# An attention and snake-MLP kernel: the order of the first loads and products

## The chip, the cores and the metric

The kernel runs on one core of one Trainium2 chip. The metric is device time in microseconds: the median of several runs. A core has TensorE (PE, matrix products; its weight loads are listed as PEld), VectorE (DVE), ScalarE (ACT), GpSimd (POOL) and SyncE (SP). SyncE, ScalarE and GpSimd can issue DMA transfers. In the profile, q1 is the DMA queue that SyncE fills and q0 the one that GpSimd fills.

## The reference

Linear attention over 8 batches, 8 heads, 576 positions and 64 features a head, followed by a layer of 512 to 2048 to 512 features with a "snake" activation over all 4608 positions:

```python
q_s = exp(q - max(q)) / sum(...)             # softmax over the 64 features
k_s = exp(k - max(k, axis=2)) / sum(...)     # softmax over the 576 positions
kv  = einsum('bhsd,bhse->bhde', k_s, v)      # 64 x 64 a head
x   = q_s @ kv                               # then heads side by side: 4608 x 512
h   = x @ w_in                               # 512 x 2048
g   = h + sin(alpha * h)**2 / (alpha + 1e-9)
out = g @ w_out                              # 2048 x 512, float32
```

All inputs and the output are float32.

## The kernel before

**Tiles.** The 4608 positions go in nine blocks `t` of 512 rows (`MF`); a batch is 576 rows, nine sub-blocks `j` of 64 (for the first block only the first eight sub-blocks of batch 0 are needed). q, k and v of a batch are staged with two heads' halves (`ii` = 0, 1) that can be loaded apart. `x` is kept transposed in `xT`, four chunks `c` of 128 features. `w_in` is in `win`, as four row blocks `ki` of 128 features by 2048 columns; a column block `ni` is 128 columns. It is loaded with a cast to bf16 on GpSimd's queue, in pieces `load_win(c0, c1, k0, k1)` of columns c0 to c1 and row blocks k0 to k1, each as two issues of 64 partitions (`x` = 0, 1).

**One block.** For each `ni`, `mm_h` accumulates four products (`ki` = 0 to 3) in a PSUM bank; ScalarE takes the sine of it (L260), one of three engines squares it, VectorE combines (L270), and `g` goes into 16 products per output tile (`mm_o`, L274). Products of block `t+1` run between those of block `t`.

**Order.** The schedule is manual: each engine runs its instructions in the order of the program text. Nothing reorders them, so an instruction that waits holds up everything behind it on its engine. DMAs of one queue are issued in the order of the text too, and an issue can wait for the eighth transfer before it on its queue.

**The opening** (all before 28 us), as the text orders it:

- L302: SyncE issues q half 0, k half 0, q half 1, v half 0, k half 1. `held` (L332) is a one-element copy on GpSimd that waits for a loaded piece (k half 0), so that what GpSimd issues behind it starts no earlier. Behind it come v half 1 in two pieces (sub-blocks 0 to 4 and 5 to 8), `win` in six column ranges of all four row blocks, and half of `w_out`.
- ScalarE: `exp_half` for q half 0, k half 0, q half 1 (L119), then the cast of v half 0 to `vb` (L329), the copy of the first transposed q (`qT`, L355), the exponential of k half 1, part of the cast of v half 1, an `xT` chunk (L370), the second `qT` copy (L371), and a load of the sine table.
- VectorE: `norm_q`: for each half of q the sums (L151), the reciprocals (L152) and the product (L153); then `kv_norm` (L184, L187), which writes `kbd`; the rest of the cast of v half 1; the other `xT` chunks (L369, L381).
- TensorE: `warm_up(n)` are n products whose result is not used (L343). Between them stand the transposes of normed q (L203), the K·V products `kv_mm` (L174) of each half, and the attention chunks `attn_chunk` (L231), whose output becomes `xT`. As soon as `xT` chunks 0 and 1 exist, `mm_h` runs row blocks 0 and 1 of the first two column blocks, then attention chunks 2 and 3, then row blocks 0 and 1 of column blocks 2 and 3. The row blocks 2 and 3 follow in `h_slot`, which goes through all column blocks.
- Later in block 0 SyncE loads batch 1 (`load_q1` at column blocks 6 and 13, `load_kv1` at 13, L420 and L428), and its v half 1 is cast on VectorE (L450).

Of the kernel before, what the change touches and what calls it, by code (L numbers as in the profile page):

```python
# [15 lines left out]
F32 = mybir.dt.float32  # L16
BF16 = mybir.dt.bfloat16
AX = mybir.ActivationFunctionType
ALU = mybir.AluOpType
AXL = mybir.AxisListType  # L20
# [3 lines left out]
def kernel(  # L24
# [14 lines left out]
    nc = tc.nc  # L39
    ctx.enter_context(nc.allow_non_contiguous_dma(reason="layout"))  # L40
    B, H, S, D = q.shape
# [3 lines left out]
    J = 9  # L45
# [11 lines left out]
    att1 = ctx.enter_context(tc.tile_pool(name="att1", bufs=1))  # L57
    att2 = ctx.enter_context(tc.tile_pool(name="att2", bufs=2))
    small = ctx.enter_context(tc.tile_pool(name="small", bufs=2))
# [18 lines left out]
    def src_view(t, b):  # L78
        return t[b].rearrange("(i e) (p j) d -> (e p) i (j d)", e=2, j=J)
# [5 lines left out]
    staged = {}  # L85
# [20 lines left out]
    def load_win(c0, c1, k0=0, k1=4):  # L106
        n, kk = slice(c0, c1), slice(k0, k1)
        for x in range(2):
            nc.gpsimd.dma_start(out=win[64 * x:64 * x + 64, kk, n], in_=win_v[x][:, kk, n])
# [5 lines left out]
    A = {}  # L115

    def exp_to(dst, src, iis=range(2)):
        for ii in iis:
            nc.scalar.activation(dst[:, :, ii * 128:(ii + 1) * 128].rearrange("p j (x d) -> p x j d", x=2),  # L119
                                 src[:, ii::2], AX.Exp)  # L120
# [2 lines left out]
        A["qe", b] = att2.tile([128, J, 4 * D], BF16, name="qe")  # L123
        exp_to(A["qe", b], staged["q", b])

    def exp_half(name, b, ii, j1=J):
        if ii == 0:
            A[name + "e", b] = att2.tile([128, J, 4 * D], BF16, name=name + "e")
        exp_to(A[name + "e", b][:, 0:j1], staged[name, b][:, :, 0:j1], (ii,))

    def exp_k(b):
        A["ke", b] = att2.tile([128, J, 4 * D], BF16, name="ke")
# [7 lines left out]
    def norm_q(b, engs, j1=J):  # L140

        qe = A["qe", b][:, 0:j1].rearrange("p j (ii x d) -> p ii j x d", ii=2, x=2)
        A["qn", b] = qn = att1.tile([128, 2, J, 2 * D], BF16, name="qn")
        qs = small.tile([128, J, 4], F32, name="qs")
        if len(engs) == 1:
            nc.vector.tensor_reduce(qs, A["qe", b].rearrange("p j (i d) -> p j i d", i=4), axis=AXL.X, op=ALU.add)  # L146
            nc.vector.reciprocal(qs, qs)  # L147
        for ii in range(2):
            part = qs[:, 0:j1, 2 * ii:2 * ii + 2]
            if len(engs) == 2:  # L150
                nc.vector.tensor_reduce(part, qe[:, ii], axis=AXL.X, op=ALU.add)  # L151
                nc.vector.reciprocal(part, part)  # L152
            engs[ii % len(engs)].tensor_tensor(qn[:, ii, 0:j1].rearrange("p j (x d) -> p j x d", x=2), qe[:, ii],  # L153
                                               part.unsqueeze(3).to_broadcast([128, j1, 2, D]), op=ALU.mult)
# [9 lines left out]
    def kv_mm(b, ii, pool, split=False):  # L164

        if ii == 0 or split:
            A["kvp", b] = pool.tile([128, 2, 512], F32, name="kvp", tag="a")
        kvp, ke, vt = A["kvp", b], A["ke", b], vb[b % 2]
        for j in range(J):
            for x in range(2):  # L170
                h = 2 * ii + x
                for e in range(2):
                    r = slice(64 * e, 64 * e + 64)
                    nc.tensor.matmul(kvp[64 * x:64 * x + 64, e, ii * 65:(ii + 1) * 65],  # L174
                                     ke[r, j, h * 64:(h + 1) * 64],
                                     vt[r, j, h * 65:(h + 1) * 65],
                                     start=(j == 0), stop=(j == J - 1))

    def kv_norm(b, i0=0, i1=2):

        kt, m = kbd[b % 2], i1 - i0
        kvr = small.tile([128, 2, 2], F32, name="kvr")[:, :, 0:m]
        src = A["kvp", b][:, :, i0 * 65:i1 * 65].rearrange("p e (ii c) -> p e ii c", ii=m)
        nc.vector.reciprocal(kvr, src[:, :, :, D])  # L184
        for x in range(2):
            r = slice(64 * x, 64 * x + 64)
            nc.vector.tensor_tensor(kt[r, :, i0:i1, r], src[r, :, :, 0:D],  # L187
                                    kvr[r].unsqueeze(3).to_broadcast([64, 2, m, D]), op=ALU.mult)

    def q_tile(b):  # L190
        if ("qT", b) not in A:
            A["qT", b] = att2.tile([128, 2, J, 128], BF16, name="qT")
        return A["qT", b]
# [34 lines left out]
    def attn_chunk(b, c, j0, j1, xp):  # L228

        ii, e = divmod(c, 2)  # L230
        nc.tensor.matmul(xp, kbd[b % 2][:, e, ii], A["qT", b][:, ii, j0:j1, e * 64:(e + 1) * 64],  # L231
                         start=True, stop=True)
# [7 lines left out]
    def bank(kind):  # L240

        if kind == "k":
            return ps_k.tile([128, 2, MF], F32, name="kvp", tag="a")[:, 0]
        pool = {"a": lambda: ps_h[0], "b": lambda: ps_h[1], "l": lambda: ps_l, "o": lambda: ps_o}[kind]()
        return pool.tile([128, MF], F32, name={"l": "lp", "o": "op"}.get(kind, "hp"), tag=kind)

    def mm_h(t, ni, k0=0, k1=4):

        if ni == 0 and k0 == 0:
            G[t] = gpool.tile([128, nN, MF], BF16, name="g")  # L250
        hp = HP[t, ni] if k0 else bank(BANKS.get(t, 4 * "aabb")[ni])
        HP[t, ni] = hp
        for ki in range(k0, k1):
            nc.tensor.matmul(hp, win[:, ki, ni * 128:(ni + 1) * 128],  # L254
                             xT[:, ki, t * MF % NX:t * MF % NX + MF], start=(ki == 0), stop=(ki == 3))
        return hp
# [36 lines left out]
    ACT_CP, DVE_CP, GP_CP = nc.scalar.copy, nc.vector.tensor_copy, nc.gpsimd.tensor_copy  # L293
    V, GP = nc.vector, nc.gpsimd
# [3 lines left out]
    def load0(eng, n, t, ii, j0=0, j1=J):  # L298
        eng.dma_start(out=staged[n, 0][:, ii::2, j0:j1].rearrange("p i j d -> p i (j d)"),  # L299
                      in_=src_view(t, 0)[:, ii::2, j0 * D:j1 * D])  # L300

    for n, t, ii in (("q", q, 0), ("k", k, 0), ("q", q, 1), ("v", v, 0), ("k", k, 1)):  # L302
        load0(nc.sync, n, t, ii, 0, 8 if n == "q" else J)
    nc.scalar.dma_start(out=alpha_rows, in_=moe_alpha.rearrange("(no ni) -> no ni", ni=128))
    make_identity(nc, ident)
# [23 lines left out]
        eng(vv[:, 2 * ii:2 * ii + 2, j0:j1, 0:D], staged["v", 0][:, ii::2, j0:j1])  # L329

    held = singles.tile([128, 1], F32, name="held")
    GP_CP(held, staged["k", 0][:, 0, 0, 0:1])  # L332
    load0(GP, "v", v, 1, 0, 5)
    load0(GP, "v", v, 1, 5, 9)
    for c0, c1 in ((0, 256), (256, 512), (512, 768), (768, 1024), (1024, 1536), (1536, 2048)):
        load_win(c0, c1)
    for c in range(2):
        load_wout(4 * c, 4 * c + 4)
# [1 line left out]
    def warm_up(n):  # L340

        for _ in range(n):
            nc.tensor.matmul(warm, identb, A["qe", 0][:, 0:4, 0:128], start=True, stop=True)  # L343

    exp_half("q", 0, 0, 8)
    exp_half("k", 0, 0)
    exp_half("q", 0, 1, 8)
    warm_up(7)  # L350
    norm_q(0, [V, V], 8)
    q_tile(0)
    q_transpose_ii(0, 0, 0, 8, tp0)
    cast_v0(0, 0, 9, ACT_CP)
# [1 line left out]
    exp_half("k", 0, 1)  # L356
    warm_up(2)
    kv_mm(0, 0, ps_k, split=True)
    warm_up(3)
    kv_norm(0, 0, 1)  # L360
    tp1 = ps_l.tile([128, 8, 128], BF16, name="tp", tag="l")
    q_transpose_ii(0, 1, 0, 8, tp1)
# [12 lines left out]
    for ki in range(2):  # L375
        for ni in range(2):
            mm_h(0, ni, ki, ki + 1)
    for c in range(2, 4):
        xp = bank("l")
        attn_chunk(0, c, 0, 8, xp)  # L380
        DVE_CP(xT[:, c, 0:MF], xp)  # L381
    for ki in range(2):
        for ni in range(2, 4):
            mm_h(0, ni, ki, ki + 1)

    def h_slot(t, ni, sq, lag):
        hp = mm_h(t, ni, 2 if ni < (4, 1, 0)[min(t, 2)] else 0)
# [161 lines left out]
    c0 = J * 2 * P  # L549
# [30 lines left out]
    for t in range(3, nT):  # L580
        b = t + 1 if t + 1 < B else None
# [60 lines left out]
```

## Time and profile before

| what | value |
|---|---|
| median of 3 runs | 284.21 us (284.12 to 284.5) |
| the profiled execution's own time | 283.31 us |
| its span, first to last instruction | 281.5 us |
| TensorE busy | 270.0 us, 96% |
| ScalarE busy | 225.3 us, 80% |
| VectorE busy | 188.8 us, 67% |
| GpSimd busy | 83.5 us, 30% |
| granted TensorE clock, mean | 1.000 |
| read from and written to HBM | 36.71 and 9.44 MB |

The span is what the profile shows, and 1.8 us of the profiled execution's time lie around it. Shares of busy time are means over stages; the rows of a stage say what that stage waits for. A row of the timeline is start, length, engine, line, operation, tiles written and read, form and count; a bracket at its end gives the idle time ahead of it and what ended that.

### The profile page before, as it was taken

The page shows a single profiled execution, that of the slowest core. Times are in us where ns is not written, and L with a number is a line of the kernel's source. Part 1 is how long each engine was busy: PE and PEld are TensorE (multiplying, and loading weights), DVE is VectorE, ACT ScalarE, POOL GpSimd, SP SyncE. Part 2 cuts the span into 40 slices and gives each one's busy share as a digit, 9 for nine tenths or more (in the row PEclk, how much of TensorE's full clock was granted, in tenths as well). Part 3 has the DMA queues.
Part 4 walks back from the last instruction along what each step waited for, and adds up shares of the span by engine and source line. Part 5 has one row for each costly group of instructions (what it writes and reads, how often), then busy time and mean ns, then how long its engine had stood idle before and what let it go on. Part 6 is the DMA issues. An engine that isn't in the chain of part 4 may idle for free.

```text
span 281.5 us, 4812 instructions
## 1 busy us (share of the span) xinstructions
PE 270.0 (96%) x1828; PEld 128.3 (46%) x1857; DVE 188.8 (67%) x286; ACT 225.3 (80%) x320; POOL 83.5 (30%) x80
## 2 busy tenths in 40 slices
PE   2999999999999999999999999999999999999994
PEld 1444444444444444444444444444444444444443
DVE  4968678899877768766875678577765555555412
ACT  4989477999489999899989998999877777777400
POOL 2989411877666450115003501250000000000000
PEclk9999999999999999999999999999999999999999
DMA  7999989898599039712991199109011111112143
GB/s 265 299 199 232 299 282 334 329 307 302 118 235 386 8 82 330 292 37 49 269 380 43 29 296 376 28 10 161 11 29 37 37 40 37 37 37 45 42 103 75
DMA packets 39127, 45.80 MB, mean 163 GB/s; under 512 B 17072, under 2 KB 22464, under 8 KB 39104
## 3 DMA queue, kind: packets, MB, share of 16 engines
q1 hardware_dynamic: 33360, 40.57, 47.2%
q0 software_dynamic: 5552, 4.79, 10.2%
q8 instruction: 14, 0.23, 0.3%
q10 hardware_dynamic: 192, 0.14, 0.2%
q14 instruction: 9, 0.07, 0.1%
HBM read 36.71 MB, written 9.44 MB: 164 GB/s over the span
## 4 chain that ended last, share of the span: by engine, by line
PE 85%; DMA 7%; POOL 2%; DVE 2%; issue 1%; ACT 1%; SPq 1%; ACTq 0%
PE op L274 38%; PE hp L254 37%; DMA st_v<-in_v_dram 4%; PE xp L223 2%; DMA win<-in_moe_w_in_dram 2%; DMA st_k<-in_k_dram 2%; PE kvp L174 2%; PE lp L254 2%; POOL s L264 1%; PE op L612 1%; PE op L254 1%; ACT s L260 1%; PE kvp L254 1%; POOL st_v L299 1%; DVE g L270 1%
## 5 line engine op out<-in xcount | busy, mean ns | idle before, releaser
L270 DVE SCALAR_TENSOR_TENSOR g<-s,inva_sb,hp 128x512 bf16<-128x512 f32 x128 | 94.1, 745 | 58.1 <-ACT s L262 52.6
L254 PE MATMUL hp<-xT,win 128*128 128x512 bf16 x507 | 127.7, 379 | 0.7 <-DMA win<-in_moe_w_in_dram 0.5
L274 PE MATMUL op<-wout,g 128*128 128x512 bf16 x477 | 121.6, 379 | 1.4 <-issue 0.6
L260 ACT ACTIVATE s<-hp,alpha_sb 128x512 f32<-128x512 f32 x128 | 86.2, 682 | 23.1 <-PE hp L254 22.3
L254 PEld LDWEIGHTS <-win 128*128 128x128 bf16 x576 | 56.0, 98 | 67.7 <-issue 1.3
L274 PEld LDWEIGHTS <-g 128*128 128x128 bf16 x560 | 54.0, 98 | 61.0 <-DVE g L270 0.3
L262 ACT ACTIVATE s<-s 128x512 f32<-128x512 f32 x112 | 70.5, 630 | 3.5
L264 POOL TENSOR_TENSOR s<-s 128x512 f32<-128x512 f32 x29 | 30.4, 1063 | 20.1 <-ACT s L260 20.0
L153 POOL TENSOR_TENSOR qn<-qe,qs 128x1152 bf16<-128x1152 bf16 (+1 forms) x12 | 25.1, 2110 | 33.6 <-DVE qs L147 22.3
L286 DVE COPY o<-op 128x512 f32<-128x512 f32 (+2 forms) x33 | 22.1, 669 | 9.9 <-PE op L274 5.5
L138 POOL CAST vb<-st_v 128x1152 bf16<-128x1152 f32 x12 | 14.4, 1233 | 46.0 <-DMA st_v<-in_v_dram 32.0
L119 ACT ACTIVATE qe<-st_q 128x1152 bf16<-128x1152 f32 (+1 forms) x16 | 17.5, 1130 | 5.8 <-DMA st_q<-in_q_dram 5.6
L119 ACT ACTIVATE ke<-st_k 128x1152 bf16<-128x1152 f32 x16 | 17.9, 1151 | 1.3 <-DMA st_k<-in_k_dram 1.3
L146 DVE TENSOR_REDUCE qs<-qe 128x36 f32<-128x2304 bf16 x5 | 12.8, 2553 | 7.9 <-ACT qe L119 7.9
L226 DVE CAST xT<-xp 128x512 bf16<-128x512 f32 (+1 forms) x18 | 13.5, 751 | 0.0
L151 DVE TENSOR_REDUCE qs<-qe 128x16 f32<-128x1024 bf16 (+1 forms) x6 | 7.5, 1252 | 4.9 <-ACT qe L119 4.9
L119 ACT ACT_TABLE_LOAD x7 | 9.0, 1283 | 1.3 <-PEq L626 1.2
L274 PE MATMUL lp<-wout,g 128*128 128x512 bf16 x31 | 8.8, 379 | 0.2 <-issue 0.2
L274 PE MATMUL hp<-wout,g 128*128 128x512 bf16 x30 | 8.6, 380 | 0.1
L223 PE MATMUL xp<-qT,kbd 128*128 128x256 bf16 (+1 forms) x40 | 8.2, 286 | 0.0
L187 DVE TENSOR_TENSOR kbd<-kvp,kvr 64x256 bf16<-64x256 f32 (+1 forms) x20 | 7.4, 369 | 0.5
L174 PEld LDWEIGHTS <-ke 64*64 64x64 bf16 x576 | 5.7, 106 | 4.2 <-ACT vb L329 1.1
(83 smaller groups left out, 135.3 us busy)
## 6 DMA issues: line engine op xcount, KB each, us to landing
out_dram<-o SPq DMA_DIRECT2D x70, 128.0 KB, 2.4
st_q<-in_q_dram SPq DMA_DIRECT2D x6, 1152.0 KB, 6.6
st_k<-in_k_dram SPq DMA_DIRECT2D x6, 1152.0 KB, 8.7
st_v<-in_v_dram SPq DMA_DIRECT2D x6, 1152.0 KB, 11.5
st_k<-in_k_dram SPq DMA_DIRECT2D x4, 576.0 KB, 7.1
st_q<-in_q_dram SPq DMA_DIRECT2D x4, 512.0 KB, 5.7
st_v<-in_v_dram SPq DMA_DIRECT2D x3, 576.0 KB, 7.9
wout<-in_moe_w_out_dram POOLq DMA_DIRECT2D x3, 512.0 KB, 10.3
```

Of the source, the lines that this page charges most:

```text
L119: nc.scalar.activation(dst[:, :, ii * 128:(ii + 1) * 128].rearrange("p j (x d) -> p x j d", x=2), src[:, ii::2], AX.Exp)
L138: engs[ii](vv[:, 2 * ii:2 * ii + 2, :, 0:D], staged["v", b][:, ii::2])
L153: engs[ii % len(engs)].tensor_tensor(qn[:, ii, 0:j1].rearrange("p j (x d) -> p j x d", x=2), qe[:, ii], part.unsqueeze(3).to_broadcast([12 ...
L223: nc.tensor.matmul(xp[:, e, 0:n], kt[:, e, ii], qT[:, ii, j0:j1, e * 64:(e + 1) * 64], start=True, stop=True)
L226: eng(xT[:, 2 * ii:2 * ii + 2, c0:c0 + n], xp[:, :, 0:n])
L254: nc.tensor.matmul(hp, win[:, ki, ni * 128:(ni + 1) * 128], xT[:, ki, t * MF % NX:t * MF % NX + MF], start=(ki == 0), stop=(ki == 3))
L260: nc.scalar.activation(s, hp, AX.Sin, scale=alpha_sb[:, ni:ni + 1])
L262: nc.scalar.activation(s, s, AX.Square)
L264: nc.gpsimd.tensor_tensor(s, s, s, op=ALU.mult)
L270: nc.vector.scalar_tensor_tensor(G[t][:, ni], in0=s, scalar=inva_sb[:, ni:ni + 1], in1=hp, op0=ALU.mult, op1=ALU.add)
L274: nc.tensor.matmul(acc, G[t][:, ni, j * 128:(j + 1) * 128], wout[:, ni, :], start=(ni == 0), stop=(ni == nN - 1))
L286: eng(o[:, cols], acc)
```

## The change

Four edits in the opening.

- v half 1 of batch 0 becomes the sixth load on SyncE's queue, as one transfer, and leaves GpSimd's. GpSimd's gate waits for q half 1 rather than k half 0.
- The first 512 columns of `win` are loaded by half of the row blocks: row blocks 0 and 1 of columns 0 to 255, the same of columns 256 to 511, then row blocks 2 and 3 of columns 0 to 511. The other columns stay as they are.
- The exponentials of each q half of batch 0 are taken in two parts of four sub-blocks, and the sums (new `norm_q0`) in the same parts; reciprocal and product stay one instruction a half.
- On TensorE the second group of warm-up products behind the first K·V products is one instead of three, and row block 0 of column blocks 2 and 3 stands ahead of attention chunks 2 and 3.

```diff
-    def exp_half(name, b, ii, j1=J):
-        if ii == 0:
+    def exp_half(name, b, ii, j1=J, j0=0):
+        if (name + "e", b) not in A:
             A[name + "e", b] = att2.tile([128, J, 4 * D], BF16, name=name + "e")
-        exp_to(A[name + "e", b][:, 0:j1], staged[name, b][:, :, 0:j1], (ii,))
+        exp_to(A[name + "e", b][:, j0:j1], staged[name, b][:, :, j0:j1], (ii,))
...
-    for n, t, ii in (("q", q, 0), ("k", k, 0), ("q", q, 1), ("v", v, 0), ("k", k, 1)):
+    for n, t, ii in (("q", q, 0), ("k", k, 0), ("q", q, 1), ("v", v, 0), ("k", k, 1), ("v", v, 1)):
         load0(nc.sync, n, t, ii, 0, 8 if n == "q" else J)
...
-    GP_CP(held, staged["k", 0][:, 0, 0, 0:1])
-    load0(GP, "v", v, 1, 0, 5)
-    load0(GP, "v", v, 1, 5, 9)
-    for c0, c1 in ((0, 256), (256, 512), (512, 768), (768, 1024), (1024, 1536), (1536, 2048)):
+    GP_CP(held, staged["q", 0][:, 1, 0, 0:1])
+    for c0, c1, k0 in ((0, 256, 0), (256, 512, 0), (0, 512, 2)):
+        load_win(c0, c1, k0, k0 + 2)
+    for c0, c1 in ((512, 768), (768, 1024), (1024, 1536), (1536, 2048)):
         load_win(c0, c1)
...
-    exp_half("q", 0, 0, 8)
+    qe0 = A["qe", 0] = att2.tile([128, J, 4 * D], BF16, name="qe")
+    qn0 = A["qn", 0] = att1.tile([128, 2, J, 2 * D], BF16, name="qn")
+    qs0 = small.tile([128, J, 4], F32, name="qs")
+
+    def norm_q0(ii):
+        part = qs0[:, 0:8, 2 * ii:2 * ii + 2]
+        src = qe0[:, 0:8, ii * 128:(ii + 1) * 128].rearrange("p j (x d) -> p j x d", x=2)
+        for j0 in (0, 4):
+            nc.vector.tensor_reduce(part[:, j0:j0 + 4], src[:, j0:j0 + 4], axis=AXL.X, op=ALU.add)
+        nc.vector.reciprocal(part, part)
+        nc.vector.tensor_tensor(qn0[:, ii, 0:8].rearrange("p j (x d) -> p j x d", x=2), src,
+                                part.unsqueeze(3).to_broadcast([128, 8, 2, D]), op=ALU.mult)
+
+    for j0 in (0, 4):
+        exp_half("q", 0, 0, j0 + 4, j0)
     exp_half("k", 0, 0)
-    exp_half("q", 0, 1, 8)
+    for j0 in (0, 4):
+        exp_half("q", 0, 1, j0 + 4, j0)
     warm_up(7)
-    norm_q(0, [V, V], 8)
+    norm_q0(0)
+    norm_q0(1)
...
     kv_mm(0, 0, ps_k, split=True)
-    warm_up(3)
+    warm_up(1)
     kv_norm(0, 0, 1)
...
             mm_h(0, ni, ki, ki + 1)
+    for ni in range(2, 4):
+        mm_h(0, ni, 0, 1)
     for c in range(2, 4):
         xp = bank("l")
         attn_chunk(0, c, 0, 8, xp)
         DVE_CP(xT[:, c, 0:MF], xp)
-    for ki in range(2):
-        for ni in range(2, 4):
-            mm_h(0, ni, ki, ki + 1)
+    for ni in range(2, 4):
+        mm_h(0, ni, 1, 2)
```

## The prediction

> **What bounds the kernel now.** First the page's head and engine totals, then the rows of TensorE, ScalarE and VectorE in the opening, then the chain of waits further on, then the DMA queues by stretch.
>
> The page says what sets the end: TensorE is busy for 270.0 of 281.5 us. Its idle time lies nearly all ahead of 13.3 us.
>
> ```profile
> span 281.5 us, 4812 instructions
> PE 270.0 (96%) x1828; PEld 128.3 (46%) x1857; DVE 188.8 (67%) x286; ACT 225.3 (80%) x320; POOL 83.5 (30%) x80
> ```
>
> The timeline of TensorE (start, length, engine, line, operation, tiles, count, and in brackets the idle time before and what ended it):
>
> ```profile
> 5.46 3.15 PE L343 MATMUL warm<-qe,identb 128*128 128x512 bf16 x7 [2.14 <-ACT qe L119]
> ...
> 9.26 0.94 PE L343 MATMUL warm<-qe,identb 128*128 128x512 bf16 x2
> ...
> 10.53 0.82 PE L343 MATMUL warm<-qe,identb 128*128 128x512 bf16 x3
> ...
> 12.33 0.48 PE L174 MATMUL kvp<-vb,ke 64*64 64x65 bf16 x36
> 13.31 0.81 PE L254 MATMUL hp<-xT,win 128*128 128x512 bf16 x3 [0.50 <-DMA win<-in_moe_w_in_dram]
> 14.17 0.59 PE L231 MATMUL lp<-qT,kbd 128*128 128x512 bf16 x2
> 14.77 2.83 PE L254 MATMUL hp<-xT,win 128*128 128x512 bf16 x12
> ```
>
> The one stall in it that a load ends is 0.50 us at 13.31, for w_in's first 256 columns. (Four products stand there; one record is missing.) From there TensorE starts a 512-column product every 0.216 us with few breaks. The rows of ScalarE and VectorE show what else the start of that stream needs:
>
> ```profile
> 10.49 1.16 ACT L119 ACTIVATE ke<-st_k 128x1152 bf16<-128x1152 f32 x1
> 11.55 0.72 ACT L329 CAST vb<-st_v 128x640 bf16<-128x640 f32 x1
> ...
> 12.86 1.02 ACT L371 COPY qT<-tp 128x1024 bf16<-128x1024 bf16 x1
> ```
> ```profile
> 13.07 0.59 DVE L187 TENSOR_TENSOR kbd<-kvp,kvr 64x128 bf16<-64x128 f32 x2
> 14.59 1.29 DVE L381 CAST xT<-lp 128x512 bf16<-128x512 f32 x2 [0.93 <-PE lp L231]
> ```
>
> ScalarE has no gap from 8.52, when v's first half has landed, to 12.27. VectorE's two casts of the last xT chunks end at 15.88, and the first column block's last product (w_in's fourth row block) starts behind them at 15.93. Then the chain of waits from 28 us on (start, length, what):
>
> ```profile
> 31.10 10.03 DMA st_v<-in_v_dram
> ...
> 41.16 0.76 DVE vb L450
> 41.95 0.69 DVE xT L468
> 42.65 0.60 DVE qT L458
> ...
> 44.00 0.60 PE hp L231 x2
> ```
>
> This is a second gate, far behind the edit: v of batch 1 lands at 41.13, VectorE works without a gap to 43.94, and TensorE's products at 44.00 start then. Did TensorE arrive earlier, it would wait here. And that landing is a matter of bytes; the DMA answer for 2 to 41 us has its engines busy in every slice, by two queues in turn (q1 is SyncE's, q0 GpSimd's):
>
> ```profile
> DMA  8999999999999999999999999999999999999997
> ...
> q0 software_dynamic: 5527, 4.76, 73.6%
> q1 hardware_dynamic: 2984, 6.21, 41.8%
> ```
>
> **The parts of the change.**
>
> *Exponentials and sums of q in parts.* ScalarE's row for 1024 columns takes 1.06 us and for 1152 columns 1.16, so 0.83 ns a column and 0.2 fixed: a part of 512 takes 0.63, two of them 1.2. That adds 0.15 us to each half of q on ScalarE, in time that it idles for loads (0.44 ahead of 5.85; 0.35 ahead of 8.52, where 8.18 becomes 8.33 and the cast still waits for v at 8.50). Cost nothing; without those gaps, 0.3 us. VectorE begins its sums at about 5.02 instead of 5.45. Two sums of 0.66 (1.22 for 1024 columns, 1.04 ns a column by the 2.55 us row for 2304) replace 1.22, so the first norm ends near 7.9 instead of 8.22, the second near 10.75 instead of 10.98. Behind the second stand kbd and the first xT chunks: 0.15 to 0.2 earlier, and through them ScalarE's qT copy ends at 13.72 rather than 13.88. The first gain goes nowhere: ScalarE's first qT copy at 9.59 follows the cast of v.
>
> *Warm-up.* The seven products wait for the first part alone, so they run from about 5.03 to 8.0. Three later ones become one: at the 0.216 us of that stage 0.43 less, in front of transposes that wait for the norm anyway. Nothing on the path in this execution.
>
> *v's second half on SyncE's queue.* It is the sixth issue there, near 3.3 us, 0.5 us long, with nothing behind it until 22.98. The halves of k and v on that queue land 1.43 apart (v's first 8.50, k's second 9.93), so 11.36. Now the two GpSimd pieces land at 10.8 and 11.4. ScalarE's cast can start at 11.55 in both. Zero, with 0.2 us of margin, if w_in's packets keep behind v's. The evidence for that is this stretch, 6.9 to 9.1 us:
>
> ```profile
> q1 hardware_dynamic: 409, 0.91, 104.2%
> ```
>
> GpSimd issued v from 6.00 on, and until SyncE's queue was through on an engine (9.2) not one packet of q0 ran. But from 26.6 to 28.4 us, with both queues filled, they do share:
>
> ```profile
> q1 hardware_dynamic: 232, 0.46, 69.7%
> q0 software_dynamic: 134, 0.12, 41.3%
> ```
>
> There SyncE's queue gets 0.46 MB in 1.8 us, 256 GB/s instead of 412. I take no sharing, as the first row is of the same stage, with SyncE's descriptors issued long before; the other end is the rival below. The Trainium skill (DMA: Bandwidth & Descriptors, Queues, rings and completion order) has each DMA engine go round robin between the queues that have work, packet by packet: this speaks against the change, and the later row agrees with it, the earlier does not. By that rule v would land a microsecond late and the sum would be the slow rival's.
>
> *The gate and w_in.* GpSimd now waits for q's second half (1.77 + 5.3 = 7.07) instead of k's first (5.83), then starts w_in at 7.25 instead of 7.62, since the two v issues (1.63) are gone. All six issues for the first 512 columns are out before v is through. The bytes ahead are the same, so the stream starts when it did. Blocks of 128 KB landed 0.68 us apart (12.49, 13.17, 13.96, 14.63), those of 256 KB, with 512 columns, 1.28 (0.64 per 128 KB). The first pieces are half as large: row blocks 0 and 1 of columns 0 to 255 land near 12.49 instead of 13.17, of columns 256 to 511 near 13.17 instead of 14.63, and the rest near 14.55. Whole stream: 4 x 0.68 = 2.72 becomes 4 x 0.34 + 2 x 0.64 = 2.64, so 0.08 us shorter.
>
> *Products reordered.* The K·V products are issued by 12.65 in both (they hang on ScalarE's cast, 12.27). Then 4 + 2 products of 0.216 run from 12.66 to 13.95, both waits for w_in covered. The attention chunks, next in order, find qT (13.72) and kbd (13.66) ready and start at 13.95 instead of 14.17. VectorE's two casts follow as they did, 0.42 behind, so 15.66 instead of 15.88, and the last product of the first column block starts near 15.71 instead of 15.93. The 0.50 stall is gone, but 0.25 and 0.42 now stand ahead of the third and fourth row block: those casts are late next. Had the two hoisted products stood behind the chunks, these could start at 13.75; the reorder itself gives 0.2 back.
>
> **Sum.** The opening brings 0.22 us. At 44.00 it meets v of batch 1, which comes only 0.08 us earlier (same bytes, engines never idle, slightly faster blocks), and TensorE waits out the other 0.14. Behind that nothing is touched. Net −0.1 us on the profiled 283.31 (span 281.5 and 1.8 around it), so 283.2 there; the median of the runs is 0.9 above it, and the same step from 284.21 gives 284.1. A measurement of this kernel tells 0.2%, 0.57 us, from no change.
>
> **Rivals.**
>
> *Slower: v's second half shares with w_in.* Place: ScalarE's cast at 11.55. If q0 gets packets from about 8.9 us (its first issue 7.25 plus the 1.64 us that an issue at 36.91 took to its first packet), 0.82 MB are left for SyncE's queue; at 256 GB/s they take 3.2 us and v lands near 12.5. It decides from 11.55 on, each microsecond later costing one: cast, K·V, norm, chunks, then TensorE, which also arrives at 44.00 late by as much less the 0.2 that the opening gained. About +0.8 to +1.0, so 285.0 to 285.2. For it: the later stretch. Against it: the early one.
>
> *Faster: the usual execution is later in its opening than the profiled one.* The median is 0.9 above it, and the clock may be why: products of 512 columns are 0.43 apart up to 9.68 and 0.22 from 10.53. If the switch comes at 12 us, the three warm-ups, transposes and chunks ahead of the K·V products run at the slow spacing: three warm-ups 1.28 instead of 0.65, eight transposes 0.85 instead of 0.45, and TensorE comes to 15.93 about 0.9 later, past the second gate, so all counts. The changed order has two warm-ups less (0.86 at that spacing) and starts 0.43 earlier: it gets 0.6 to 0.9 back, 283.3 to 283.6. For it: the 0.9. Against it: that difference may lie anywhere, the loads of batch 1 included, and the runs lie within 0.4. The Trainium skill (TensorE: Matmul & The Clock Gate, Part 1) counts the warm-up in time, about 3.4 us in a free-running window; the trace has 4.5 from 5.46 to about 9.9, which allows both.
>
> *The second gate doesn't hold* (the batch 1 load moves up with its earlier issue): the 0.22 stays, 284.0, no change within measurement.
>
> **How the numbers follow.** Gate holds or not, the effect is −0.1 to −0.2: 0.50, its own range 283.7 to 284.6. Faster rival 0.27, slower rival 0.23. A range of 283.3 to 285.0 takes in the faster one's worth and most of the slower one's.
>
> **What would show it.** Right: no idle for w_in on TensorE after the K·V products; chunks near 13.95 and their casts' end near 15.7; ScalarE's cast of v still at 11.55; v of batch 1 near 41.05, products behind it near 43.9. Wrong: that cast starting after 11.6 (the load shares), TensorE waiting for w_in, or a landing near 41 that moves by over 0.3 either way.

## The result, and the profile after

The changed kernel takes 286.42 us (median of 6 runs, 285.71 to 287.57), the kernel before 284.36 us beside it (6 runs, 283.77 to 285.34). The ratio is 1.0067, interval 1.0041 to 1.0092: slower by some 2 us, where 284.1 had been forecast, with 285.0 as the upper end. The profiled execution took 286.07 us.

First the page's head and engine totals of the changed kernel.

```profile
span 284.3 us, 4814 instructions
PE 269.3 (95%) x1826; PEld 127.6 (45%) x1855; DVE 188.7 (66%) x288; ACT 225.5 (79%) x322; POOL 83.7 (29%) x80
```

The work is the same within a microsecond on every engine; the span is 2.8 us longer. So the loss is waiting. The chain of waits of the changed kernel, from its start to the loads of batch 1 (start, length, what), says for whom:

```profile
1.76 6.17 DMA st_q<-in_q_dram
...
7.98 0.52 POOL held L332
8.50 3.07 POOL win L109 x5
11.57 5.49 DMA win<-in_moe_w_in_dram
...
17.19 0.61 PE hp L254 x2
17.82 1.85 ACT s L260 x3
...
32.05 8.61 DMA st_v<-in_v_dram
```

Read it forward. q's second half lands at 7.93 and opens the gate; then GpSimd makes five issues of w_in one after the other; the sixth (row blocks 2 and 3 of columns 0 to 511, second half of the partitions) takes 5.49 us from its issue to its landing, and TensorE's products behind it start the column blocks. Neither the issues nor that landing stood on the path in the prediction's opening. The column blocks being late, SyncE issues the last five loads of batch 1 later too (from 31.12 on, before from 29.15), and the chain goes on over the *first* half of batch 1's v, which lands at 40.66, where the prediction's chain had the second half.

TensorE's timeline of the changed kernel (start, length, engine, line, operation, tiles, count, and in brackets the idle time ahead and what ended it):

```profile
13.59 0.48 PE L174 MATMUL kvp<-vb,ke 64*64 64x65 bf16 x36 [0.78 <-ACT vb L329]
14.00 1.47 PE L254 MATMUL hp<-xT,win 128*128 128x512 bf16 x5
15.31 0.59 PE L231 MATMUL lp<-qT,kbd 128*128 128x512 bf16 x2
...
17.19 1.89 PE L254 MATMUL hp<-xT,win 128*128 128x512 bf16 x8 [0.85 <-DMA win<-in_moe_w_in_dram]
```

The first pieces of w_in are there in time (no bracket at 14.00), the last one is not. GpSimd's rows, the kernel before and then the changed one, show the queue that brings them:

```profile
6.00 1.63 POOL L299 DMA_DIRECT2D st_v<-in_v_dram  x2
7.62 4.96 POOL L109 DMA_DIRECT2D win<-in_moe_w_in_dram  x8
```
```profile
7.98 0.52 POOL L332 COPY held<-st_q 128x1 f32<-128x1 f32 x1 [6.67 <-DMA st_q<-in_q_dram]
8.44 8.06 POOL L109 DMA_DIRECT2D win<-in_moe_w_in_dram  x13
```

Eight issues of 128 KB took 4.96 us before (0.62 each); the thirteen now, four of them of 64 KB, six of 128 and three of 256, take 8.06 (also 0.62). An issue costs GpSimd the same whether it moves 64 or 128 KB: in the changed kernel's trace both start 0.58 to 0.61 us apart. And they start at 8.44, not at the 7.25 of the prediction.

What the queue delivers, as stretches (window, length, busy time and count of PE, PEld, DVE, ACT, POOL, then granted clock, DMA share, GB/s), before and then changed:

```profile
13.00:16.00 3.00, 2.63 (x11) 1.10 (x13) 1.90 (x5) 2.36 (x3) 2.65 (x5) 1.00 1.41 185
16.00:20.00 4.00, 4.00 (x20) 1.78 (x19) 2.42 (x4) 3.63 (x7) 3.12 (x4) 1.00 1.26 199
```
```profile
13.00:16.00 3.00, 2.36 (x45) 1.26 (x45) 1.94 (x6) 2.98 (x4) 3.00 (x6) 1.00 1.02 117
16.00:20.00 4.00, 3.15 (x16) 1.30 (x15) 2.44 (x4) 2.61 (x6) 2.96 (x5) 1.00 1.28 178
```

The last column is what matters: 117 GB/s instead of 185 for 3 us is 204 KB less, 178 instead of 199 for 4 us another 84 KB. At the rates of before these 288 KB are 1.1 + 0.4 = 1.5 us. Two things go together here. Fewer packets are in flight: the DMA share is 1.02, before 1.41 (it counts packets that overlap, so that it can exceed 1). And single packets take long: of the packets of q0 that start between 13 and 16 us, 8 took over 1.4 times their usual time (the median of packets of their size) before, 1.5 us too much in all, and 53 in the changed kernel (12.0 us too much, up to 1.25 us on one packet that usually takes 0.1).

Last, the second gate. VectorE's cast of batch 1's v, before at 41.16, in the changed kernel:

```profile
43.59 0.76 DVE L468 CAST vb<-st_v 128x1152 bf16<-128x1152 f32 x1
```

It moved by 2.43 us. From it to the end of the span are 240.7 us; before, 281.5 − 41.16 = 240.3. Nearly the whole loss, 2.4 of 2.8 us, is thus in front of that cast. By an estimate from the bytes about 1.5 us of it is the stretch from 13 to 20 us. Another 0.6 to 0.85 would belong to loads ahead of any edit (q's first half landed at 4.94 instead of 4.33, v's first at 9.35 instead of 8.50 in this execution); a second profile of the same kernel below (e11) is late by less there, and its cast stands at 43.11. The total agrees: by 20 us the kernel before had moved 5.13 MB, the changed one 4.74, e11 4.81, and at 200 GB/s those gaps are 1.9 and 1.6 us.

### The profile page after: what moved, and what is told of

Read it like the earlier page. It is cut to its first block, busy times and chain, and to the rows that moved or that the text cites. A ratio compares the mean times of both kernels' runs of the same rounds, so it can differ in the third digit from the quotient of the medians.

```text
span 284.3 us, 4814 instructions
## 1 busy us (share of the span) xinstructions
PE 269.3 (95%) x1826; PEld 127.6 (45%) x1855; DVE 188.7 (66%) x288; ACT 225.5 (79%) x322; POOL 83.7 (29%) x80
## 3 DMA queue, kind: packets, MB, share of 16 engines
q1 hardware_dynamic: 33632, 41.16, 47.5%
## 4 chain that ended last, share of the span: by engine, by line
PE 83%; DMA 7%; POOL 3%; ACT 2%; DVE 1%; issue 1%; SPq 1%; ACTq 0%
PE op L274 37%; PE hp L254 36%; DMA st_v<-in_v_dram 3%; DMA st_q<-in_q_dram 2%; POOL s L264 2%; DMA win<-in_moe_w_in_dram 2%; PE kvp L174 2%; PE xp L223 2%; DVE g L270 1%; PE op L630 1%; PE op L254 1%; PE lp L254 1%; ACT s L260 1%; POOL win L109 1%; PE kvp L254 1%
## 5 line engine op out<-in xcount | busy, mean ns | idle before, releaser
L119 ACT ACTIVATE qe<-st_q 128x1152 bf16<-128x1152 f32 (+2 forms) x18 | 17.7, 1025 | 7.2 <-DMA st_q<-in_q_dram 7.1
L174 PE MATMUL kvp<-vb,ke 64*64 64x65 bf16 x576 | 6.7, 194 | 2.4 <-ACT vb L329 1.7
L109 POOL DMA_DIRECT2D win<-in_moe_w_in_dram x14 | 8.7, 669 | 0.8 <-DMA win<-in_moe_w_in_dram 0.8
```

## The experiments

Sixteen kernels, in four groups. A ratio is that to the kernel before on the same chip, with its 95% interval. Two handles turned out to matter, the point at which GpSimd's gate opens and the size of a w_in issue. Their cells:

| w_in's first 512 columns | gate: k half 0 | gate: q half 1 |
|---|---|---|
| four issues of 128 KB, all rows (before) | 1; e13 0.9996; e10 1.0001 | e9 1.0027; e1 1.0027 |
| four of 64 KB, two of 128 KB (the change) | e2 1.0036; e12 1.0033; e3 1.0045 | changed 1.0067; e11 1.0059 |
| four of 128 KB by half of the row blocks | e15 1.0025; e14 1.0017 | e5 1.0012; e7 1.0015 |

(v's second half goes by SyncE in e1, e5, e7, e9, e11, e12, e13 and e14, by GpSimd in e2, e3, e10 and e15. Kernels of one cell differ in other parts of the change: exponentials, warm-ups, order of the products.)

### Which part of the change costs: e1 to e4

Theory: small issues starve the queue. Rivals: v's move to SyncE's queue costs, or the last pieces are merely too coarse.

**e1**, the change but w_in in pieces of all row blocks:

```diff
-    for c0, c1, k0 in ((0, 256, 0), (256, 512, 0), (0, 512, 2)):
-        load_win(c0, c1, k0, k0 + 2)
-    for c0, c1 in ((512, 768), ...):
+    for c0, c1 in ((0, 256), (256, 512), (512, 768), ...):
```

> The changed kernel, with w_in in full row blocks as before (v still on SyncE's queue). In the changed kernel's profile GpSimd's queue moved only 0.35 MB from 13 to 16 us (117 GB/s; before 179 GB/s over 11 to 17), and row blocks 2 and 3 of the first columns landed at 17.05. Theory A, the half-row pieces are what is slow: the queue is back at 180 to 190 GB/s behind v, the first full piece lands near 13.2 to 13.9, the time falls by 1.3 to 2 us to about 284.6. Theory B, v on SyncE's queue is the cause (w_in starts later against the other queue): the slow stretch stays and the time stays at 286 to 286.5.

284.07 us, 1.0027 (1.0012 to 1.0042). More than half of the loss is gone. The first stretch is back at full rate:

```profile
13.00:16.00 3.00, 2.31 (x10) 0.95 (x12) 1.55 (x5) 2.30 (x3) 3.00 (x6) 1.00 1.44 192
```

What is left, 0.27%, is in this profile TensorE's own: the hoisted products wait 0.55 us, until 14.36, for the second column range, which lands at 14.22 behind all row blocks of the first. The cast of batch 1's v is at 41.26, as before.

**e2**, the kernel before with only w_in's three pieces of the change:

```diff
-    for c0, c1 in ((0, 256), (256, 512), (512, 768), ...):
+    for c0, c1, k0 in ((0, 256, 0), (256, 512, 0), (0, 512, 2)):
+        load_win(c0, c1, k0, k0 + 2)
+    for c0, c1 in ((512, 768), ...):
```

> The kernel before, with only w_in's half-row pieces. Theory A: the slow stretch appears here too, the time rises by 1.3 to 2 us over the kernel before (285.7 to 286.3). Theory B: no slow stretch, the wait of 0.50 us for w_in is gone, time within 0.3 us of the kernel before.

284.59 us, 1.0036 (1.0011 to 1.006): 1.1 us, where 1.3 to 2 were expected. The pieces alone slow the kernel, with the earlier gate, v on GpSimd's queue and the old product order. The slow stretch comes with them:

```profile
13.00:16.00 3.00, 2.40 (x28) 0.99 (x13) 2.23 (x6) 2.70 (x4) 2.84 (x5) 1.00 1.14 119
```

**e3**, the change with v's second half and the gate as before:

```diff
+    GP_CP(held, staged["k", 0][:, 0, 0, 0:1])
+    load0(GP, "v", v, 1, 0, 5)
+    load0(GP, "v", v, 1, 5, 9)
```

> The changed kernel, with v's second half and the gate back on GpSimd's queue as before (w_in stays in half-row pieces). Theory A: slow stretch stays, ScalarE's cast of v starts near 11.6 instead of 12.8, time 285.5 to 286.3. Theory B: time back near 284.4, no slow stretch.

284.53 us, 1.0045 (1.0026 to 1.0063; the kernel before is at 283.45 here): taking v off SyncE's queue and opening the gate earlier cures a third at most, and the intervals overlap. 13 to 16 us moved 125 GB/s, in a profiled execution that took 286.38 us, 1.8 above its median.

**e4**, the change with its third piece cut in two, so that all eight issues are of 64 KB:

```diff
-    for c0, c1, k0 in ((0, 256, 0), (256, 512, 0), (0, 512, 2)):
+    for c0, c1, k0 in ((0, 256, 0), (256, 512, 0), (0, 256, 2), (256, 512, 2)):
```

> The changed kernel, with row blocks 2 and 3 of the first 512 columns in two pieces of 256 columns (same size as the pieces ahead of them). If the 512-column half-row shape alone is slow: landing of the last of the four near 15, time 1 to 1.7 us below the changed kernel. If every half-row piece is slow or the cause lies elsewhere: as the changed kernel within 0.5 us, 286 to 286.9.

286.65 us, 1.0118 (1.01 to 1.0137). Finer pieces double the loss and prolong the slow stretch:

```profile
13.00:16.00 3.00, 2.59 (x11) 1.02 (x13) 2.04 (x5) 2.35 (x3) 3.00 (x6) 1.00 1.10 112
16.00:20.00 4.00, 2.98 (x14) 1.21 (x14) 1.44 (x2) 3.30 (x6) 3.61 (x6) 1.00 1.18 135
```

64 KB (65.5 thousand bytes) every 0.61 us is 107 GB/s: about what arrived. The trace shows the queue run dry issue by issue. From the end of an issue to its first landing on any DMA engine are 2.80 us for the first, then 2.54, 2.30, 2.06, 1.81 and 1.56; these six land 0.34 to 0.36 us apart, as fast as the engines drain 64 KB. The seventh and eighth land 0.66 and 0.83 apart. The rival of pieces that are too coarse falls; the number of issues is the cost. Nor is it the shorter rows: e1's first pieces have the same 256 columns in issues of 128 KB, and 192 GB/s.

### Issue size and issue time: e5 to e8

If the number of issues is the cost, row halves in full-size issues should be nearly free, and GpSimd starting earlier should cure the small ones.

**e5**, the change with `for c0, c1, k0 in ((0, 512, 0), (0, 512, 2))`: the same bytes in four issues of 128 KB.

> The changed kernel, with the first 512 columns in two row halves of 512 columns each (four issues of 128 KB instead of four of 64 KB and two of 128 KB). GpSimd takes 0.59 to 0.63 us to issue a piece, whatever its size, and the engines drain 64 KB in 0.35 us and 128 KB in 0.68. Theory A1, the small pieces let the queue run dry: no slow stretch, the queue moves 180 to 195 GB/s from 13 to 16 us, first halves landed near 13, time 1.2 to 2 us below the changed kernel, ratio to the kernel before 0.998 to 1.003. Theory A2, reading half of the row blocks is slow in itself: slow stretch as in the changed kernel, ratio 1.005 to 1.01.

284.05 us, 1.0012 (1.0002 to 1.0023). **e7** is e5 with the product order of before (both row blocks behind the chunks):

> As the kernel with two row halves of 512 columns, with attention chunks 2 and 3 back ahead of the products of column blocks 2 and 3. If the hoisted products only push the chunks back: the last product of the first column block starts 0.2 to 0.4 us earlier than in that kernel, time 0.1 to 0.4 us less. If the order doesn't matter: equal within 0.1 us.

284.04 us, 1.0015 (1.0005 to 1.0025). The first sine starts at 16.88 in e5 and at 16.35 in e7; the times are alike. VectorE's cast of batch 1's v shows why, in e5 and then in e7:

```profile
41.48 0.76 DVE L468 CAST vb<-st_v 128x1152 bf16<-128x1152 f32 x1 [0.23 <-DMA st_v<-in_v_dram]
```
```profile
41.43 0.76 DVE L467 CAST vb<-st_v 128x1152 bf16<-128x1152 f32 x1
```

Half a microsecond between the two orders is swallowed by batch 1's loads, as the prediction said of its 0.22: from 28 us on e7's chain of waits runs over v's first half, e5's has no load in it before 41 us.

**e8**, the change with the gate on q's first half:

```diff
-    GP_CP(held, staged["q", 0][:, 1, 0, 0:1])
+    GP_CP(held, staged["q", 0][:, 0, 0, 0:1])
```

> The changed kernel, with the gate at q's first half (landing near 4.3 instead of 7.1 to 7.9), so the small pieces are issued 2.8 to 3.5 us earlier. A1: the lead stays above 3 us, no slow stretch from 13 to 16 us, time 1 to 2 us below the changed kernel, unless w_in's packets now run among those of k and v and delay ScalarE's casts. A2: slow stretch stays, time as the changed kernel.

285.29 us, 1.0058 (1.0039 to 1.0077). w_in's first issue stands at 4.65, and the slow stretch is gone (the row of 13 to 16 us), but ScalarE's cast of v is late:

```profile
13.00:16.00 3.00, 2.00 (x43) 1.19 (x44) 1.91 (x5) 2.83 (x4) 3.00 (x6) 1.00 1.36 194
```
```profile
13.16 0.74 ACT L329 CAST vb<-st_v 128x640 bf16<-128x640 f32 x1 [1.21 <-DMA st_v<-in_v_dram]
```
```profile
q1 hardware_dynamic: 142, 0.30, 73.7%
q0 software_dynamic: 116, 0.06, 36.2%
```

The last two are e8's queues from 9 to 10.2 us (packets, MB, share of the engines' time): with both filled they share. So the prediction's slow rival is a real mechanism, at a gate that lets w_in start 3.8 us earlier than in the change; one loss is exchanged for another.

**e6**, e1 with the gate on k's second half (`staged["k", 0][:, 1, 0, 0:1]`), w_in's first issue at 10.93:

> The full-row kernel with v on SyncE's queue (ratio 1.0027), with GpSimd's gate at the landing of k's second half, near 10 us instead of 7.1 to 7.9. A1 (what counts is how far the issues are ahead of the engines): the lead, 3.0 us from the end of an issue to its first landing, falls below 2 and stalled packets and a stretch under 150 GB/s appear with full pieces too; beyond the idle gap of about 0.5 us behind v the stream loses another 0.5 to 1.5 us; ratio 1.006 to 1.012. A2: only the gap, full rate behind it; ratio 1.004 to 1.006.

289.23 us, 1.0198 (1.0157 to 1.024). TensorE idles 2.88 us for w_in until 16.00, and then the granted clock falls (see the end), so the size, above the 1.012 that was expected at most, is not the wait's alone. The direction holds with full-size issues: a later start costs.

### The other parts, and the change once more: e9 to e12

**e9**, the kernel before with v's second half on SyncE's queue and the gate on q's second half, nothing else:

> The kernel before, with only v's second half on SyncE's queue and the gate at q's second half (w_in in full row blocks, products and exponentials as before). If the move is free, as predicted: ratio 0.999 to 1.001, ScalarE's cast of v near 11.6, w_in's first block landed near 13.2. If the move is part of the loss: ratio 1.002 or more and the cast or the first block later.

284.14 us, 1.0027 (1.0012 to 1.0042). The opening is not disturbed; it is the later stretch that is thinner (178 GB/s, before 199):

```profile
13.00:16.00 3.00, 2.75 (x12) 1.16 (x12) 2.06 (x6) 2.44 (x4) 3.00 (x6) 1.00 1.43 187
16.00:20.00 4.00, 4.00 (x20) 1.86 (x19) 2.56 (x4) 3.77 (x7) 3.44 (x5) 1.00 1.22 178
```

VectorE's cast of batch 1's v is at 41.95, 0.8 later than before.

**e10**, the kernel before with only q's exponentials and sums in parts (`exp_half` and `norm_q0` of the change, three warm-ups and the old order kept):

> The kernel before, with only q's exponentials and sums in two parts (loads, warm-ups and products as before). Predicted to cost and bring nothing on the path: ratio 0.999 to 1.001, second norm ending 0.2 us earlier. If the split delays ScalarE's casts: 1.001 to 1.002.

283.53 us, 1.0001 (0.999 to 1.0013). Its second norm runs from 9.58 to 10.81 (predicted end 10.75, before 10.98), and none of that reaches the end. Free, as predicted.

**e11** is the changed kernel itself on this chip:

> The changed kernel itself, on the chip of the others of this call. Ratio 1.004 to 1.009 again; if the first loads' late landing in its first profile (4.94 us instead of 4.33 to 4.66) was of that execution alone, they land near 4.5 here, and the time is 0.3 to 0.6 us less against the kernel before, while the slow stretch stays; if it belongs to the change, they are late again.

285.26 us, 1.0059 (1.0038 to 1.008). v's cast is at 11.81 here, so not late, and still TensorE waits, longer than in the first profile:

```profile
14.31 0.59 PE L231 MATMUL lp<-qT,kbd 128*128 128x512 bf16 x2
17.19 1.89 PE L254 MATMUL hp<-xT,win 128*128 128x512 bf16 x8 [1.86 <-DMA win<-in_moe_w_in_dram]
```

The late v of the first profile was therefore not the cause. The last of the six pieces lands at 17.05 in both.

**e12**, the change with the gate back on k's first half:

```diff
-    GP_CP(held, staged["q", 0][:, 1, 0, 0:1])
+    GP_CP(held, staged["k", 0][:, 0, 0, 0:1])
```

> The changed kernel, with the gate back at k's first half (landing near 5.9 instead of 7.1 to 7.9). The gate at 4.5 gave no slow stretch but v landed at 13.1; the gate at 7.1 gave the slow stretch. If the lead is what counts, this is between: 13 to 16 us at 140 to 185 GB/s, v landed by 12.2, ratio 1.002 to 1.005. If there is no such trade, the ratio is that of the changed kernel.

284.38 us, 1.0033 (1.0013 to 1.0054). The gate gives back 0.9 us of 1.84 (285.26 to 284.38, same chip), though the two intervals overlap. The profiled execution took 285.57 us, 1.2 above its median. In it 13 to 16 us is at 188 GB/s, but between 16 and 20 there are 33 stalled packets (7.5 us too much), TensorE waits 0.40 us for a later piece at 21.60, and the cast stands at 43.15 (before: 2 such packets, 0.75 us). Issued 2 us earlier, the small pieces pass; what stalls is the stretch behind them.

### Gate against move, and row halves alone: e13 to e16

**e13**, e9 with the gate on k's first half, so that v's move stands alone:

> The kernel before, with v's second half on SyncE's queue and the gate left at k's first half (the same move with the later gate cost 1.0027). If the later gate, not the move, cost that: ratio 0.999 to 1.001, full rate through 20 us. If the move itself costs: 1.002 to 1.004 again.

283.38 us, 0.9996 (0.9979 to 1.0013). v's move is free; e9's 0.27% belongs to the gate. Its profiled execution, 285.41 us, is 2 us above its median (the first loads slipped and v landed at 13.74 beside w_in), so that trace is not read for the rest.

**e14**, e7 with the gate on k's first half, and **e15**, the kernel before with only `((0, 512, 0), (0, 512, 2))` for the first 512 columns:

> Row halves of 512 columns, chunks first, gate at k's first half: the changed kernel with the three things mended that the runs so far blame. If they are all: ratio 0.998 to 1.000. If v's move costs in itself: 1.0015 or more.

> The kernel before, with the first 512 columns in two row halves of 512 columns (128 KB an issue, as before). The small pieces alone cost 1.0036. If only their size mattered: 0.999 to 1.001, no stretch under 170 GB/s, and, with the last gate at batch 1's v, no gain either. If row halves cost in any shape: 1.002 or more.

283.94 us, 1.0017 (1.0009 to 1.0026), and 284.17 us, 1.0025 (1.0008 to 1.0042). Both miss the value hoped for. Of the other branches e13 excludes e14's (v's move), and e15's holds: row halves cost 0.5 to 0.7 us even at full issue size and with the early gate. In e15 w_in's first piece is late (TensorE waits 1.04 us until 13.97, before 0.50 until 13.31), and from 11 to 13 us 144 GB/s move instead of 167. Why is open.

**e16**, the kernel before with only the gate moved to q's second half, v still on GpSimd's queue behind it:

```diff
-    GP_CP(held, staged["k", 0][:, 0, 0, 0:1])
+    GP_CP(held, staged["q", 0][:, 1, 0, 0:1])
```

> The kernel before, with only GpSimd's gate moved from k's first to q's second half, so its issues start 1.3 us later; v's pieces still reach an engine only when SyncE's queue is through, so they land as before. If the lead of the issues is what counts: ratio 1.001 to 1.004, stalled packets from 16 to 20 us, batch 1's v later by 0.3 to 1 us. If it doesn't: 0.999 to 1.001.

286.49 us, 1.0119 (1.0076 to 1.0161), above the 1.001 to 1.004 expected. Here GpSimd issues v first, so w_in starts at 9.82, 2.2 us later than before; v too lands later (12.37 instead of 11.40), which the expectation had ruled out. TensorE waits for w_in:

```profile
15.23 1.02 PE L254 MATMUL hp<-xT,win 128*128 128x512 bf16 x4 [2.04 <-DMA win<-in_moe_w_in_dram]
```

Of the six executions three, with a mean granted clock of 0.998 to 1.000, took 285.8 us, 0.8% more than before; two with 0.986 and 0.992 took 288.6 and 289.8, and one with 0.998 took 287.1. So a later gate with v left on GpSimd's queue is dear (0.8%); with v moved away it is cheap (e9, 0.27%).

### What they say together

With the issues of before, the later gate costs 0.27% (e9; e13 without it 0; e1 has the same figure, with the wait of the hoisted products in it). Row halves in small pieces with the early gate cost 0.33 to 0.36% (e2, e12; e3 0.45). Sum 0.60 to 0.63; measured 0.59 and 0.67. But the two don't simply add: in the table's third row, row halves in full-size issues, the later gate costs nothing (0.12 to 0.15% with it, 0.17 to 0.25 without). Issue size is shown best with the later gate, at the same bytes: eight small issues 1.0118, four small and two full ones 1.0059 and 1.0067, four full ones 1.0012, with intervals apart. With the early gate, e2 and e12 against e15 and e14, the intervals overlap. The exponentials and v's move cost nothing (e10, e13). No kernel beat the one before beyond its interval.

A way to read both handles at once is GpSimd's lead: from the end of an issue to its first landing on any engine, taken at the issue whose landing then spreads.

| kernel | lead, us | that issue's landings spread over, us |
|---|---|---|
| e1 (fifth and sixth issue) | 3.3 | 0.4 |
| before (sixth) | 3.8 | 0.84 |
| e9 (fifth) | 2.9 | 1.1 |
| e10 (fourth) | 3.6 | 1.3 |
| e15 (first; seventh) | 3.6; 4.1 | 1.3; 2.5 |
| e2 (sixth) | 2.5 | 2.1 |
| e5 (fifth and sixth) | 3.3 | 1.2 |
| e16 (first; fourth) | 2.4; 3.2 | 1.4; 2.1 |
| changed (sixth) | 2.1 | 2.8 |
| e11 (sixth) | 2.4 | 2.8 |
| e4 (eighth) | 1.9 | 1.3 |

Small issues eat the lead (0.62 us to issue, 0.35 to drain; e4 loses about 0.25 us an issue), a later gate starts with less of it. e5 and e4 show this by the size alone, e12 and e16 by the start alone. The lead doesn't explain all: e5 has e1's lead and spreads more, in e12 the larger pieces behind the first six stall with 3.8, e15 stalls with 3.6 and 4.1, and e10 spreads over 1.3 us at no cost in time. Shown is that small issues let the queue run dry (e4) and that time is lost where the issues are made smaller, or come later with the issues of before; that the lead is what makes packets stall is argued. Open stays what stalls a packet inside, and the 0.1 to 0.25% that row halves cost at full issue size.

## Why the prediction was wrong

**The failed step** is "The gate and w_in". It said: "All six issues for the first 512 columns are out before v is through. The bytes ahead are the same, so the stream starts when it did", and made the stream 4 x 0.34 + 2 x 0.64 = 2.64 us, 0.08 shorter than before. Three terms of it were wrong.

- *The start.* Predicted first issue at 7.25, measured 8.44 (e11 8.09). q's second half landed at 7.93 (e11 7.36), not 7.07, and the gate's copy itself held GpSimd for 0.52 us (e11 0.74, before 0.19 by its row): at the new place it ends only when a product on VectorE does (see the end). The sixth issue ended at 12.20 (e11 11.85), after the 11.36 at which v was to be through, and the first piece was late (12.96 and 13.15 for 12.49; e11 12.00 and 12.33).
- *The supply.* The step took 0.34 us for 64 KB from the engines' side. It had all six issues out by 11.36, but in the length of the stream it never asked what GpSimd needs for them. The row `7.62 4.96 ... x8` of before would have told it: 0.62 us an issue. At 0.62 for 0.34 of transfer the queue drains faster than it fills.
- *The end.* Row blocks 2 and 3 were put at 14.55; they landed at 15.08 and 17.05 (e11 14.36 and 17.05). This alone makes TensorE idle 0.85 us (e11 1.86) at 17.19, where the step had no wait at all, and the bytes lost behind it shift batch 1's loads.

The Trainium skill (DMA: Bandwidth & Descriptors, Issuing engines are not separate DMA queues) calls the time of issuing a DMA usually small relative to the DMA. It is not so here: 0.61 us of issue beside 0.35 us for 64 KB, and e4 is 1.2% slower for it.

**What held.** *Exponentials in parts cost nothing*: e10, 1.0001. *v's move costs nothing*: e13, 0.9996; its landing was given as 11.36 with the cast at 11.55, and the cast came at 11.81 in e11, 12.80 in the first profile. *No wait for w_in after the K·V products*: true of the first six hoisted products. *Chunks at 13.95*: 14.31 in e11 (cast late by 0.26), 15.31 in the first profile. *The second gate*: it held in the main. From that cast to the end are 240.3 to 240.8 us before, after, and in e2, e3, e5, e7, e8, e9 and e11 (e1 241.0), and e5 against e7 shows half a microsecond of product order vanish in it. But the chain runs over that cast only in some profiles (before, e3, e11, e12); in the changed kernel's first profile, e4, e7 and e9 it runs over v's first half and its cast on ScalarE, and in e1, e2 and e5 no load stands in it from 28 to 41 us. And the landing, predicted at 41.05, came at 43.56 and 43.08: a gate "of bytes" passes on bytes that are lost ahead of it, and this was used only for the 0.08 us gained.

**The rivals.** *Slower, v shares with w_in*: the sign was right, the mechanism not this one. It decides only when the gate opens much earlier (e8: cast at 13.16). With the change's gate the cast in e11 is 0.26 us late, and e12 with a gate 2 us earlier than e11 has the cast at 11.81 too. *Faster by the clock*: no run showed it. In the 18 profiles the clock is at full speed from 7.9 to 11.2 us on, never as late as the 12 of the rival; the warm-ups were not tried alone. *The gate doesn't hold*: its landing moved, but not up as that rival had it.

The rival that was missing is one mechanism: GpSimd's issues as the bound of its own queue. From before's rows it is 0.62 − 0.34 = 0.28 us for each of four small issues, 1.1 us; the later start (8.09 and 8.44 against 7.62) adds 0.5 to 0.8. Together that is 1.6 to 1.9 of the 1.8 to 2.1 us measured. This is an estimate made afterwards: it leaves out the lead that covers the first small issues, and what row halves cost by themselves.

## What to carry to other kernels

Price a DMA edit on both sides, by what the issuing engine needs for an issue and by what the engines need for its bytes; if the issue takes longer, smaller pieces make the stream slower as soon as the queue has no lead left, however much earlier the first is wanted. A gate that holds back a queue has two wrong sides, sharing with what it protects (e8) and a queue that runs without lead (e16), and moving it needs both looked at. And where a later load gates everything, a gain ahead of it vanishes, while bytes lost ahead of it arrive there in full.

## What the runs showed of the hardware that was not expected

**The clock can fall after a short idle.** In e16's profile TensorE idles 2.04 us ahead of 15.23. The rows behind it:

```profile
16.00:20.00 4.00, 3.20 (x10) 0.92 (x8) 1.29 (x2) 0.00 (x0) 2.69 (x5) 0.53 1.31 175
20.00:24.00 4.00, 4.00 (x13) 1.47 (x12) 2.17 (x3) 2.90 (x5) 1.87 (x3) 0.62 1.24 204
```

The granted clock is 0.53 and 0.62: by the trace it is 0.50 from 16.22 to 23.05, 6.8 us in all, and 1.00 on either side. The profiled execution took 288.64 us, three at a mean clock of 0.998 to 1.000 took 285.8, so the same program doesn't always lose the clock. e6, with 2.88 us idle, shows the same 0.53; e11 with 1.86 us idle does not (1.00 from 16 to 20).

The Trainium skill (TensorE: Matmul & The Clock Gate, Part 1) lets the clock drop after at least one idle window of about 3.4 us. In this execution 2.04 us were enough, so the measurement decides: a stall of two microseconds in the opening can cost as much again in clock. That the idle time is the cause is read from two profiles; no run varied it alone.

**An issue costs GpSimd a fixed time.** 0.62 us for 64 KB as for 128 KB (8.06 us for 13 issues, 4.96 for 8).

**A copy on GpSimd waits for a product on VectorE.** The gate's copy of one element a partition, before and then in the changed kernel beside what VectorE does meanwhile:

```profile
5.88 0.19 POOL L332 COPY held<-st_k 128x1 f32<-128x1 f32 x1 [4.57 <-DMA st_k<-in_k_dram]
```
```profile
7.23 1.23 DVE L358 TENSOR_TENSOR qn<-qe,qs 128x1024 bf16<-128x1024 bf16 x1
```

The product ends at 8.46, the copy, begun at 7.98, at 8.50. In all nine profiles where the copy falls into such a product it ends some 0.05 us behind it and takes 0.52 to 1.10 us (e9 1.10); in the other nine, beside VectorE's sums or nothing, it takes 0.19. So 0.3 to 0.9 us of the later gate's start is this wait, not the landing it waits for. No run takes the two apart: e9's 0.27% may be its cost.

**A few DMA engines can fall behind and hold up a whole piece.** The sixth issue of the changed kernel lands on its first DMA engine at 14.28 and on its last at 17.05; the two behind it still spread over 1.9 us, where e1's spread over 0.4. In e11 fourteen of sixteen landings are there by 15.74 and the last two come at 16.77 and 17.05; for both issues behind it two landings are again a microsecond behind the rest. Small issues are not needed for it (in e15, with issues of 128 KB, the seventh spreads over 2.5 us), so a starved queue is not shown to be its cause.
